# Attention and token/channel mixer on one core: a shorter opening in one PSUM bank, bfloat16 fillers, the identities behind the first load, and batch 2's second token product in seven products

## The chip, the cores and the metric

The kernel runs on one core of one Trainium2 chip. The metric is the device time of one execution in microseconds; the lower the better. Where several runs are shown, the median counts.

## The reference

The inputs are q, k, v (8 batches, 8 heads, 1024 positions, 64 features), E and F (64 x 1024) and four weights of a mixer. In fp32:

```
k_proj = E @ k;  v_proj = F @ v                     # per batch and head: 64 x 64
attn   = softmax(q @ k_proj.T / sqrt(64))           # 1024 x 64
x      = heads of (attn @ v_proj) side by side      # 1024 x 512 per batch
h      = relu(x.T @ w_tok1) @ w_tok2                # token products: 1024 -> 256 -> 1024
u      = x + h.T
out    = u + relu(u @ w_ch1) @ w_ch2                # channel products: 512 -> 1536 -> 512
```

## The kernel before

All products run in bfloat16 with fp32 sums in the eight PSUM banks. Loads by GpSimd (POOL) turn fp32 into bfloat16 on the way.

**Stages.** For a batch there is a front and a back. The front: `kv_proj` (line 509) multiplies k and v by E and F, `k_transpose` and `q_transpose` turn what the scores need, `scores` (line 613) gives q·k and its exp goes to `a` on ACT (line 622), `attend` (line 636) multiplies by v, and DVE divides by the sum (lines 648 and 653). Then come the first token product (`token1...`), the second (`token2...`) with x added on DVE to give u, and the turning of u. The back: `up_set` (line 1172, three sets in each half batch) and `down_block` (line 1281). The channel products use the seven-product scheme of Strassen and Winograd: seven products of quarters for eight, with sums of weights and operands on DVE and ACT copies of a PSUM bank that seed the next sum.

**The second token product in three forms.** Batch 0 works by pairs of heads (`token2_part`). Batch 1 uses eight plain sums of 512 columns (`token2`, lines 727 and 738). From batch `TWO = 2` on, `token2` calls `token2_two`: rows by two, 4 times 4 products of 512 columns (line 752) and a DVE sum of 1024 elements (line 765). From batch `T2 = 3` on the form is `token2_seven`: four DVE differences of 256 (line 961) and two sets, each with seven pairs of products of 256 columns (line 983), one ACT copy (line 1025) and six DVE sums of 512 (lines 1013 and 1019). It needs four sums of weights, `tok2_sums` (line 935), which are made after the back of batch `T2 - 1`.

**The order.** Every piece of work is a job of a planner, with an engine, its reads and writes and its PSUM bank. The planner does not choose: the order of all jobs is written out by hand in the string `ORDER` (two characters a job), and the bank of each in `SPOTS`. The instructions of each engine run in just this order. A job's place in it is called its place below. Loads of batch 0 are by two heads each, in the order of their jobs on POOL's queue.

**The opening.** After the zero tiles are set, PE runs ten bfloat16 products of 512 columns on zeros (`warm`, line 422), one into each bank and three into bank 7. The jobs that take a bank depend on all of these and on `identities`, which makes a bfloat16 and an fp32 identity on POOL. With the fp32 identity PE turns E and F (line 447), and ACT and DVE copy them to `EFT_sb` (line 450), which every projection needs. The tuple `FILLS` names places of PE jobs; ahead of each such job, once for each time that it is named, stands one more product on zeros, in fp32 (line 1516, two records each in the profile):

```python
FILLS = (20, 25, 25, 25, 25, 25, 25, 38)
```

Place 20 is the turning of E and F, place 25 the first projection (heads 0-1), place 38 the first score. POOL issues the loads of k 2-3, v 0-1, q 0-1 and k 0-1, makes the identities, and goes on with v 2-3, k 4-5, v 4-5, q 2-3 and so on.

Of the kernel before, what the change touches and what calls it, by code (L numbers as in the profile page):

```python
# [12 lines left out]
ACT = mybir.ActivationFunctionType  # L13
EARLY = 12.0
ORDER = (
    "0301020P0U000W0V0X0R0Q0T0Z040607050Y090S0a0b0c080d0y0z141M100+0-15110A0B1312161O1P1Q0C1N1R18171m1U19"
    "1S1A1n1o1q1B1T1p1r1D2A1J1E1C1K1V0D1t1s2C2B1F1W1Y1u1X1Z1L1v1G1H1a1j2J1d1w2G2K0E1g0F1b1c1e1k1f1l1I1y0G"
    "1x2H2I1z2D2N1h2L24271i2F2E2O1+2125282Y2629221-2V2g2M2b2h2c232P2d0I0H202W2Z2Q2R2X2S2l2i2m2e2n2q2T2a2j"
    "2o2f2k0J0K2U0N0O2v2r2z2p2w2+0L2s2t312x2u2y2-350e32393336303D370f3A3Z3r34383L0g3V3a3X3B3W0i3b3M0j3C3c"
    "3d3e3E3H0k0m3Y3s473f3g3t3v0h3x3h3i3j3F3l3u3w3y483I3G3k0n0o3m3N494B3J3z4A3O0u0l3n3Q3-4C4q4P3+3K404E4F"  # L20
    "4D4m0p4r4Q413P0M4o4G4H3R3o4n4J4u4s424I4v4R4K0v434w616562634p4L3p4x564X660w4Y4y4+4N4t646857676B0q4z0r"
    "3S3T0s45504Z4M693U6C4U6A6X4V516V6Y6T6W5A6f5844464S6U6g4-526c6h5B4W6D6i536j5D0t596Z4T5O5E6F3q6H6G6E6a"
    "6d6b6e0x6L5G6p6q4O6M6r6I4a6K5H6J5C6kAF5P6l6N4b5Q6O6m5F5S5T6v6s6x5IAH4c6w6t4e6y6u6+6n5J5V4f6-6z5R6o70"
    "4d7971735U5W7A4i76545g74757E725X775K7H4j787F7B7I7G5Y7J7N5h6R6P6SAKAJ7K7CAL7D7O7Q7P7L7R5a7M7W7T6Q7S5b"
    "7X5c5LAG4k7U5i7VAN557Y5e5d4g5Z5M5N7ZAP7bAO5l7a7c7d7fAQAR4l7e7g5m7o7k7i4h5oAS5n7p7lAI7j5r7m7n5pAXAYAZ"
    "Ab5s7hAcAa5jAj5qAd5f7vAg875t7rAkAeAhAf7w5vAoAt5w7x7yAi7tAp7zAuAqAvAwAl5x5kAM7+AmAxArAn80AyAV88AsA-7s"
    "AzB08189A+8AB57-B65uB17u8BBFB28382AUBDBG5zB38CB4BEB78P84BHB8BABIB985BJBK8QBL8E8R7qBR8TBBBM8FBCBNBUBO"
    "BS86BV8S8U8H5+8D8WBPBW8X8hBTBQBb8ZBXBYBc8i8aBZBd8GBf8JBa928IBeBg5-948K8jBhAWBi968pBl8VBj8L97Bk9A8qBm"
    "938YATBn98Bo8r8b8N8cBp9KEWEVBq605yBr999B8d8f958MEZ9C9DBs9L9OBtEb8m9E9PER8eEd8gEa9GBu8n9HEc9FBw9RBx9I"
    "ByEX9S9J9Q9M9c9N9d8oEeBz9UB+Bv9T9e8s9fB-9g9W9X8tEl8kEnEm9iEj9Y8uEY8OC1Es8lEh8w9V9hEkEoEt9j8vEp9aEqEr"  # L30
    "C3C5C6C49k8x8+C9CAEu8-C7C89lEvEwCC9mEg8yC29nEzCDE+F0E-9u908z9oF19vCFCBExCJ9wEyC09pCKA0Ei9ZEf9qCEF2F3"
    "9sF4CHCIA1CLF5F6CN9zF7IaFA9rCMCO9+A2CQFBF8F9FC9-FDCbCRCPCGFE9tCSA3DEFFCcA4CVFGFH9b9xA5FI9yCTCfA7FJFK"
    "CgA6FLCdDGCWFPCiABA8DIIdCXFNFOA9DHCeFMCjCUDJFQETFRChFTFSCYFUDFCkDMACFVFZFWFXDNClESCnFaADFYFdIhCmAAIZ"
    "FhFbFeCoFcDPCtFfEUCZCpFiIgDKFkFmIeFjCuDODLFlCrDQCqCvFoDSIfFnC-DTCyD0FwFgFpDRFrFqDUFt91FxD1CzDWFzFsFu"
    "DoDVCsFyCwDXDaF-DYF+C+IbDbDZG1D2G0DdG2G3D3CaG4G6DpG5DsIiFvDqG7DcG9DeDgIrIsIpDfIqCxD4GBDiDtDrD6InDjIo"
    "DhD7IwDvDwIxItD5DADuGDIcI-DkGAIuD8IvDBGEIyDxGFIzI+DyGHJ1DCJ2J3J0IlGGGIDzGCD+D-E0E4GKE5GLE6J4J6E2J7Dm"
    "GNGRGJE9J8GMGOJ9JAGSEAGPJBIjJ5DlJCECD9JEAEJDEDJGGVJFGQEBJHJIEEDnGXG8GWEFE1GYJJGTGUGZJKEGGjJLE3GkGaEH"
    "E7JMImJNE8JOGnGoEJGdGbGqJPJRJSGeHNEIGcJTJUEKHMELIkMhJVGpGlJWJQGfHOHQJYGmGrJZGsENJXJdGvJaMjMiJbJeMkJc"
    "EOGtMmMdMeJlGgJhGwJfG-HRJiEPGhHSJjJgHPJmMgGuMfHTDDEMMlJoGxH0JkJqGiJnHUH1HWGzJpH4JsHVHXJrJtJ+H5JvHYGy"
    "JuJwJ-H7HaHbJxK1H8HZH2JyH9H6K2HeK0HcJzK3HfHAHgK5K4HdHiHBK6HwHjHhG+HCK7K8HlH3MnMoMpKAK9KDHxKBHmH+HkHo"  # L40
    "KFMrHEH-MtHnHqI1HrHDMsHpMuKHHyKGHFMxI2HsMyHzKEMzHII0KIKJMvI3M+KLI6MwM-KKHGI7HJI4KMN0N3ICHKN1N2HuKON4"
    "N8HHI8IAKPEQIDN5KCI5IEI9KRKVKNN6N7KQIHN9NDNAKSIINBNCIKKWNINEILKTNJIJIBHtHvNFKXINIMKUNGNHKnKZIOIFNKKo"
    "IPKaMqKYLQNLNMIGQhKcKrKdNNKpKbIRKsNONPNQIQNRNSISIVKeLSNXKuQiKfITKvNYKqKgQlNTNVNZNWLRNULTNaIWKhKtQmNc"
    "NdKiKwIXLUKxIUNbLVNeKjNhKzQnKyQoK+NfKlNgNiLWL3NlK-NjNpLYL4NmNkNnLXNqNsO2QpL1NuNrLaL2NtNvQkLZNwQjNoL5"
    "LbNxNyO3L8O7O5LcQqNzLeN-LdL9N+LfLgO0LiO4O6LBLALjO9O1KkLmLkOAL0OBLCOCLnLpLELqIYHLKmOEO8LFLlOFR2LsLoLD"
    "LGL6QzR3ODQxLIQvLtOHLJLhQ+LrQwQyL+LuLKQ-OLR0L-M0M1M2R1OJR4LvL7M3R5R6LHQrQtLLM4M5OMR9RARBM6OPLMOQM7ON"
    "OSMGMAM8OIMBOOR7LNMCOKM9R8MERCOZMHRDLwLORERFRGOTORMIOaOVLyOUMDOGMORHMPOdOWRIObOeRJMLOXMQOgPURKRLMFRO"
    "OrOYLxOcQuRMRPRQMMMNMJOsRNRROtOhMROjMSRSRTLzMTOfRUQsUmOiMKMVRVOlOuOvRWMUOwOkOmUlRbMWRXOyPYRZRcMZRaMX"
    "RdOxRePZUpOnOzRYOpRgUqRhPWRfPaO+UtRlUsRmUrMYPcRiPVP1OoRjO-RkPXRpMaRnP2PdRtRqOqRoP7RrMbRsP3PbP0UoS6Ru"
    "P8PfRwPeP5P9S7RyRxPCRzMcPgR+PhPFRvPkUuR-PiP4PDS0S1LPS3PGS9PjSBPmPlPES4SAPIPnS2P6UnSDS8PoPqPAPJSCSESF"  # L50
    "SGPrPpPtSIPBUzPHQ2PuU+Q3PwSJSHPsUvUxPxUyUwPKPLQ4Q6PMQ7S5U-PvQ5SLSPV0PyV1SQQ9PNV4QAPzSMPOV5PQQCQ8V6SN"
    "P+QKV7V2SRSTQDV8QBQEV3V9QLSUSWPRQ0SSQMVCQFSXQGVAVDVBSVQIQHSOSYQSVEQTPPVHSbVFVIVGPSVJQPSdQUVMSeScVKVL"
    "QQSKSZQRSfP-ShVOSvQVVPVQSaSgSiTYSkSwQJVNSxVRQWSzSjSlVSVTQ1S+SyQNVUT0SmQXQOVVSnSpTcQYTaVWQZT1SoVXT3Qa"
    "QdVbSqQbTdVcTBQcTeTgVZVaT4VdVYTbTZS-VfVeTfThVgQeT2VhTjVlViTkQfSrVjT5PTT6VkTmVmTqVtTnT7StVpT9TCTrVqTA"
    "VuVnTDTiTuVoTvTlSsVrTJVyTsToVsTGVwTpTxTyU6TtTHU7T+TKVzSuT8VxV+TIVvV-UATMTLW0W1TNW6W3TwW2W4T-TEW7W9TO"
    "TzWATFTQUBW5U0W8TRWBWDTPU1WEU8UDUCTUUEWFTSWCUFWGUGU9UOTVUHTTQgWLWHWPUIWQTWWNWdWeUPUJWTU2UKWOUQWIWRWf"
    "WMWUUWWgWSWWWhWVWjUXWiUMWJU4WkWXUTWlWYWZWKUUUYWnWmU3WbWvUVWaWoUZWwWpWzULUaURXZXYWcWqU5UbW+W-UNX0XcUS"
    "UdWxX1XaWrWyWsX2UcUeX3UhXdXeXgUiUfX5WtXfX4XhXBXjX6X7XkXbX9UjXCXiXuXDXmXlXGXvXoXHXyXpYAXnXwXzYBXxXJUg"
    "UkXITXYEX-X+YCY0WuYDX8Y1XqXKXMY4YFYHYGXAXNY5Y6YIXEY2YJXsXOXFXQYMY3Y8XPXRXLYSY7XSYNYOYQXTXtXUYTXVYKYU"
    "YXYLXrYYYPXWYZYVXXYaYWYdYRYiYbY9YcYlYfYgYeYqYjYkYnYmYrYsYhYoYuYvYtYp"  # L60
)
SPOTS = (
    "4217334766020247420761132347234101643701627014360774066762735213041450123142432343067765566765675675"
    "7567665777566576556567655413242211542021305213425767576575576676565577667573666650513140231414232503"
    "2032577665666567656666350675601421450140231314531504176766565656765666645267564312325051413232020302"
    "0477666765656566666745067565435152311422050530134126576676766666566675626736503245300142350321031412"
    "667767666565656666475765703552043505304132314120375"
)
# [116 lines left out]
def kernel(  # L185
# [232 lines left out]

    def blank(b):
        nc.tensor.matmul(  # L422
            b, zero, zero[:, None, :].to_broadcast([P, NJ, P]), start=True, stop=True
        )
# [1088 lines left out]
    for place, j in enumerate(plan):
        if j.eng == "PE":
            for _ in range(FILLS.count(place)):
                nc.tensor.matmul(  # L1516
                    spare, zero32, zero32[:, None, :].to_broadcast([P, NJ, P]), start=True, stop=True
                )
# [40 lines left out]
```

## Time and profile before

| | |
|---|---|
| median of 3 runs | 421.67 us (421.25 to 421.83) |
| profiled execution | 421.36 us, span 419.6 us |
| PE busy | 411.8 us, 98% |
| DVE busy | 353.0 us, 84% |
| ACT busy | 229.6 us, 55% |
| POOL busy | 66.8 us, 16% |
| chain that ended last | PE 96%, ACT 3% |
| lines of that chain | L1172 35%, L1281 35%, L867 4%, L983 4%, L509 3%; L1516 1%, L422 1% |

PE is TensorE, PEld its weight loads, DVE VectorE, ACT ScalarE, POOL GpSimd. L12 is line 12 of the kernel before. An engine's time is a sum over stages that differ; a stage is read from its own stretch of the trace. Times in the trace count from the start of the span. The records of one engine overlap a little, so the spacing of two starts says more of what an instruction costs than its length.

### The profile page before, as it was taken

The numbers are of one execution on the slowest core, as the hardware profiler recorded it, in microseconds if no ns is written. First come the engines' busy times: TensorE is split into PE (matmuls) and PEld (weight loads), VectorE is DVE, ScalarE is ACT, GpSimd is POOL, SyncE is SP. The second block draws the span as 40 slices with busy tenths as digits, with TensorE's granted clock in tenths as the row PEclk, the third lists the DMA queues.
The fourth block names the chain that finished last, engine by engine and source line by source line (L and its number), as shares of the span: only waits on it lengthen the run. The fifth ranks groups of instructions, "written<-read, shape, count | busy, mean of one in ns | idle before, by whom it ended". The sixth has DMA issues, their size and how long they took to land.

```text
span 419.6 us, 9401 instructions
## 1 busy us (share of the span) xinstructions
PE 411.8 (98%) x3830; PEld 348.6 (83%) x3830; DVE 353.0 (84%) x748; ACT 229.6 (55%) x444; POOL 66.8 (16%) x105
## 2 busy tenths in 40 slices
PE   9889999999999999999999999999999999999996
...
DVE  2169978989879899989898889989998988889685
ACT  1767895457466456663746547573736645354620
...
DMA  8999999997999779969859698859772401250314
GB/s 153 206 201 205 206 203 161 202 170 116 213 211 183 123 140 167 176 170 194 182 98 208 125 195 201 130 123 173 154 165 81 59 27 76 50 151 2 153 50 152
DMA packets 96812, 62.48 MB, mean 149 GB/s; under 512 B 62080, under 2 KB 92288, under 8 KB 96768
## 3 DMA queue, kind: packets, MB, share of 16 engines
...
q1 hardware_dynamic: 61056, 16.00, 23.6%
...
q8 instruction: 30, 0.49, 0.5%
q14 instruction: 14, 0.11, 0.1%
HBM read 59.24 MB, written 16.78 MB: 181 GB/s over the span
## 4 chain that ended last, share of the span: by engine, by line
PE 96%; ACT 3%; DVE 0%; issue 0%
PE psum L1172 35%; PE psum L1281 35%; PE psum L867 4%; PE psum L983 4%; PE psum L509 3%; PE psum L613 3%; PE psum L672 2%; PE psum L1516 1%; PE psum L422 1%; PE psum L636 1%; PE psum L1084 1%; ACT qT L605 1%; PE psum L727 1%; PE psum L1052 1%; PE psum L703 1%; PE psum L752 1%
## 5 line engine op out<-in xcount | busy, mean ns | idle before, releaser
L1281 PEld LDWEIGHTS <-G 128*128 128x128 bf16 x1344 | 130.2, 98 | 18.0
L1281 PE MATMUL psum<-wc_sb,G 128*128 128x256 bf16 x768 | 104.0, 273 | 0.0
L1172 PEld LDWEIGHTS <-wc_sb 128*128 128x128 bf16 x768 | 73.8, 98 | 10.3 <-issue 0.4
L1281 PE MATMUL psum<-wT,G 128*128 128x256 bf16 x576 | 78.3, 273 | 0.0
L1194 ACT ACTIVATE G<-psum 128x512 bf16<-128x512 f32 x96 | 57.0, 601 | 29.6 <-PE psum L1172 29.4
L1208 DVE TENSOR_TENSOR G<-G 128x512 bf16<-128x512 bf16 (+1 forms) x140 | 70.0, 515 | 0.6
L1172 PEld LDWEIGHTS <-wT 128*128 128x128 bf16 x576 | 55.8, 98 | 7.9 <-issue 0.4
L1172 PE MATMUL psum<-S,wc_sb 128*128 128x256 bf16 x384 | 57.1, 273 | 0.0
L1172 PE MATMUL psum<-uT,wc_sb 128*128 128x256 bf16 x384 | 56.4, 273 | 0.0
L1172 PE MATMUL psum<-S,wT 128*128 128x256 bf16 x384 | 56.2, 273 | 0.0
L622 ACT ACTIVATE a<-psum 128x512 bf16<-128x512 f32 x64 | 36.8, 599 | 23.7 <-PE psum L613 23.0
L1315 POOL DMA_DIRECT2D out_dram<-o x30 | 16.3, 547 | 182.7 <-DVE o L1321 133.5
L1200 ACT COPY ua<-psum 128x512 f32<-128x512 f32 x48 | 28.2, 587 | 28.3 <-PE psum L1172 28.0
L1321 DVE TENSOR_TENSOR o<-psum,u 128x512 f32<-128x512 f32 x59 | 40.1, 683 | 3.0 <-PE psum L1281 2.5
L1200 ACT COPY ub<-psum 128x512 f32<-128x512 f32 x48 | 28.3, 590 | 24.5 <-PE psum L1172 22.9
L1153 DVE CUSTOM_DVE_ANT_0 G<-psum,ub 128x512 bf16<-128x512 f32 x48 | 32.8, 684 | 8.5 <-PE psum L1172 8.5
L1215 ACT COPY psum<-psum 128x512 f32<-128x512 f32 x48 | 27.7, 577 | 19.7 <-PE psum L1172 12.1
L1153 DVE CUSTOM_DVE_ANT_0 G<-psum,ua 128x512 bf16<-128x512 f32 x48 | 32.8, 684 | 4.9 <-ACT ua L1200 3.9
L344 POOL DMA_DIRECT2D v_sb<-in_v_dram x18 | 13.4, 745 | 111.2 <-DMA uT<-u 50.3
L1172 PE MATMUL psum<-uT,wT 128*128 128x256 bf16 x192 | 28.8, 273 | 0.0
L689 DVE TENSOR_TENSOR x_sb<-psum,rdn 128x512 bf16<-128x512 f32 x40 | 27.6, 690 | 1.2
L613 PE MATMUL psum<-qT,kT 128*128 128x512 bf16 x64 | 22.3, 379 | 0.5 <-ACT kT L560 0.4
...
## 6 DMA issues: line engine op xcount, KB each, us to landing
...
```

What stands on the lines that cost most here:

```text
L613: lambda: nc.tensor.matmul(bank(bk), kT[:, h].rearrange("p c k -> p (c k)"), qT[:, h].rearrange("p j s -> p (j s)"), start=True, stop=True,),
L622: lambda: nc.scalar.activation(out=a_t[h // 2 % 2][:, h % 2], in_=bank(bk), func=ACT.Exp, scale=scale),
L689: lambda: nc.vector.tensor_tensor(out=x_sb[:, :, h * D : (h + 1) * D].rearrange("p (n c) d -> p n c d", n=2), in0=view()[:, :, :, 0:D], in ...
L867: nc.tensor.matmul(to, tok1_of(n, si), mv, start=(n == 1 and si == 0), stop=(si == NJ - 1), skip_group_check=True,)
L1153: nc.vector._custom_dve(TENSOR_ADD_SAT, out=out, in0=in0, in1=in1, s0=FMAX, s1=0.0)
L1172: nc.tensor.matmul(t[:, c, :], w1_of(n, dd, 2 * m + c), a_of(j, n, dd), start=(n in (1, 7) and c == 0 and dd == 0), stop=(c == 1 and dd == 1),
L1194: lambda: nc.scalar.activation(out=G[:, n, cs], in_=view(src), func=ACT.Relu),
L1200: 512, lambda: nc.scalar.copy(out=dst, in_=view("y")), writes=[(name, s % 2)],
L1208: 512 * len(both), lambda: f(out=G[:, n, c], in0=G[:, a, c], in1=G[:, b, c]), ps=False,
L1215: 512, lambda: nc.scalar.copy(out=view("y"), in_=view("x")), takes=[bk["y"]],
L1281: nc.tensor.matmul(to, G[:, G_OF[n], cc, t * P : (t + 1) * P], w2_of(n, cc), start=(n in opens and (t == 0 or alone) and cc == 0), stop=(c ...
L1321: 512, lambda: nc.vector.tensor_add(out=dst, in0=view(src), in1=u_of(sh, dh)),
```

## The change

- The opening has four products on zeros, two bfloat16 and two fp32, all into bank 5; only bank 5 counts as written at the start.
- The fillers are bfloat16 products on zeros, 21 of them: 1 ahead of the turning of E and F (place 6), 1 ahead of the first projection (11), 7 ahead of the turning of q 0-1 (15), 2 ahead of the projection of heads 2-3 (18), 3 ahead of the first score (30), 2 (41), 2 (60) and 3 (87) further on.
- `T2` is 2: batch 2's second token product takes the seven-product form, and `tok2_sums` follows the back of batch 1.
- `ORDER` and `SPOTS` are written anew for the whole program. Among what moves: POOL makes the identities right behind the first load; the loads come as k 0-1, v 0-1, v 2-3, q 0-1, k 2-3, q 2-3, q 4-5, k 6-7, k 4-5, v 4-5, q 6-7, v 6-7, then the token weights in the same order; of the six loads of `w_ch1` those of the second group come first; the first load of batch 1 (v) now stands ahead of the `w_ch2` loads.

```diff
 ORDER = (
...
 SPOTS = (
...
-FILLS = (20, 25, 25, 25, 25, 25, 25, 38)
+FILLS = (6, 11, 15, 15, 15, 15, 15, 15, 15, 18, 18, 30, 30, 30, 41, 41, 60, 60, 87, 87, 87)
 WHOLE = 3
 TWO = 2
 T1 = 2
-T2 = 3
+T2 = 2
...
-        done, held, clean = set(), {}, [True] * 8
+        done, held, clean = set(), {}, [i == 5 for i in range(8)]
...
-    def blank(b):
-        nc.tensor.matmul(
-            b, zero, zero[:, None, :].to_broadcast([P, NJ, P]), start=True, stop=True
-        )
-
-    def warm(i):
-        return pe(
-            1, 512,
-            lambda: blank(banks[i]),
-            prio=-200, writes=[("bank", i)],
-        )
-
-    opening = [warm(i) for i in (*range(8), 7, 7)]
+    def blank(z):
+        nc.tensor.matmul(
+            banks[5], z, z[:, None, :].to_broadcast([P, NJ, P]), start=True, stop=True
+        )
+
+    def warm(z):
+        return pl.add("PE", 0.43, 0.43, lambda: blank(z), prio=-200)
+
+    def warm32():
+        return pl.add("PE", 1.71, 1.71, lambda: blank(zero32), prio=-200)
+
+    opening = [warm(zero), warm(zero), warm32(), warm32()]
+    for j in opening:
+        j.mms = 1
...
-    spare = banks[5]
     for place, j in enumerate(plan):
         if j.eng == "PE":
             for _ in range(FILLS.count(place)):
-                nc.tensor.matmul(
-                    spare, zero32, zero32[:, None, :].to_broadcast([P, NJ, P]), start=True, stop=True
-                )
+                blank(zero)
             pin()
```

More of the change, by code (lines that the diff above doesn't have):

```diff
@@ L15 @@
 ORDER = (
[L16 to L60, printed above, removed]
+    "0P0Q0R0S000T0W0X010U0V0s0402030+0t0u1G050w0v080x0-1H0z0y1I1J1012091O06071114151P1L1o0A1M1K0B1N1S2413"
@@ new lines @@
+    "1p1T0C0D251Q0E161R261g1A171D1h1j1X181E1B2A1i1C190H0I2D1F0G1k2C2B1l1Y1Z1m1n1s1U2E1V1W1q1a1d2H1b1t2F1r"
+    "1c1e2G1f271u28291v1+211x2V2a2W1w1y1-20222b2I1z2P2Q232J2X2f2c2Y2g2K2R2L2d2M0F0J0K3K2h2S2e2i2k2t2l2N2T"
+    "2U2Z2O2u2p2j2m332n2o2q340L0N2v2x0c2y2r2-3B2z302s2w3F310d2+323T3U3l350Y0Z363P0a413R3Q0e3V3W3X3C0b3G3S"
+    "3r373Y3m3D3a0g383n3b3p3Z3o3q3E3d3c39423s0h3t0i3f3g3u3H3J3e0M433A0f4547463I443v504g483x4J0O494B4i3w3y"
+    "4A0j3z3h4h4C4k4l5x5y515-4D5+4m3j3-4E0k4o4K4p5z4L520o4F0l0m4j0p544n553L4r4R60570q534S3M4H614s653N4T4q"
@@ new lines @@
+    "6258634t66644u4O566R6S6N6O6P4w4P6T594x3i4Q6U6V675C3+4v3k4G6B5I3O6Z4U6Q686W4M696a5D6A6C5J6L6M6J6F6D4V"
+    "6E406X6G6b6Y4y0r0n6c6H6I5M6d4W4I4N6e5A5N6h6mAAA96n4Y6i6f6o5K6j6p6g6k6u6l6v4Z5P6r6w4X6s6q4z5B5Q706x6t"
+    "6y5O4c5L6z73745R715S5a6+72787B6-5E5T755b4d79767A7C777D7E7H5UAI6K7I5c5i7F7J7G7K7L7N7Q7M7O7R7P5FAB5G7S"
+    "AL4e4a7V5V5WAK5Y5Z5H4+AP5j7W5X7T7XAM7UAN7YAO5f7Z7e5g7g7a7iAH7f5h7h7c7d5dAJ5l5k7j4-AQAVAX5mAhAWAY4b5e"
+    "AjAi7bAZAaAb7p5nAC7q81Ae5pAT7lAc7nAkAdAfAm7r7tAgAnAoAl5q7s5oAuAxAp7u825r7wAy7kAq7mAR85B0AvAw7vArAUB1"
@@ new lines @@
+    "B25t83Az867xB584As7oAtBBBC887y7-A+B67z89BDA-B7B8B380BE7+8J878BB4BMBFB9BA8ABG8KBJ8NBNBHBK8D8LBIASBPEj"
+    "BOBLBQBSBTBR8O8CBU8Q8P5u8R8MBVBXBZEk4fBa8b8T8EBY8UBb8y90BW8cBc8SBeBd918+8VBf925vBg948W95BhBj8zBk8-AD"
+    "8X9EBi9697BlBn9F9G8FEn93988ZBm99AF8HBo8d9CBr8gBp9I8h9H9DAEBsEp8aBu8jBwAGBq9JElErEqEo9A8k5s9BC4Bv8GBy"
+    "9L8Y8e9MBxBz8lBtC5B+B-C08i9O9W8IC99P9XC7C18fC28mEs9KC3C89a8nCB9bC69N9Q8oCCEv9Y8q9ZCDCA9R9dCEF4CGCH5w"
+    "8r9c8pE-F5ExEz9e9fEm8s9g9hE+9S8u9iCN8v9j9oCJEyF0COCLCFF1CRCPCS9kF29pCQF99qFACIF39UF69mF7CbF8CU9wFBCM"
@@ new lines @@
+    "8wFCCc9xFE9tCd8tCVFDCeFG9y9TFHCtCXFFCYCu9uEwFICK9lFOFJCTCfFP9nCWEt9vCxCvCgFKFLCZCiFMFNCaDWCy9z9VFQ9+"
+    "9rChFRFSC+9-CjCkFTFUCwC-CzA1FV9sCnA2ClD0D3FWCoA0CmD9A3FXA5D1DaFYFdFZD4A6FbDYD2FcDZFaA7D5CpD6DbFeDAFf"
+    "DeDcFgFiFhEuFjDBFkD7DdDfIrFlDhFnIoA4D8IvDXFmFpDiA8In8xCrFoItIsCsFqDgDHFvDjFrFsFwIuFtDEDoFyF+DkFzDlDF"
+    "G0F-DGG1DpDmFxDIDsG2FuG3DnDJDtCqG4DKDqDvDLIpIwG8DwG9G5G6DyDuGBDMGCDCDrE4GAGFDzGDDDDODxE5GGGHD+GKG7GI"
+    "E8E9GEDNJ8E6DPD-EBGLJ9I-E7ECDQDSDREAE0EEGJJ0GRJ3J1EDEGJ4E2GNGSEFGPDTJ5J2GTEMGVIqJ6GUEHJ7GQENGWDUJAJD"
@@ new lines @@
+    "EOJBGfGgEIGYJEJCEUJFEVEKELE1GOJGJHJIERGhGjGZJJJKESEWGiEJJLJSGXGkJME3JPEPGbJTGaJNGdGmIzJQETJRGeIxJOEX"
+    "GxGMJUGcGyGnJVJWDVI+IyGlEYG-GzH0JXGpG+GoEQMsMrHaGrEZEbHeH2GqJYHcJZGsJaEcEaHfHiEfHgHbJbHjHlJcHdH3JhH5"
+    "JdJfEdHhHmJiH1HoHDJjJgJeEgH6JlJkHpJmHEMtMuJnGtGuHkH4EhGvH7JoJpH8JqHsJrJzJsJtH9HnJvHBJuMvHFHqJwJ+JxGw"
+    "HCHrK0HtHLMxK1J-K2HIK4HMEeEiK3HAMzMwK5JyHuHwKCHNK6MyHxKDK7HJHvK9HGKHKFKAHyHzHKH+KGHOK8KJKEHHM+I0I1KK"
+    "KBH-I8I2HPKLI3I9KOHQIAIEICHRKPHSKMKIIDHTM-N1KRIBIFHWN7N3HXN8IGI4N4KNIQNCIINDHUKTKUI6IHHYIRN9KVIJN5IK"
@@ new lines @@
+    "KSNAISIYNBKWHVILIMN6KZNEKXNHIZNFKbKaKcIOINNINGNJIVKdNRNSIWNKI7NLKeKfKjIXNMKhIbKgKkNNKnNOKYKlKiKmIaK-"
+    "IcNPNQI5KoNTL0KQNWNXITNUL3NVLeIdNYIPIUKqIfNZKpKrL4KtL1NaNbKsLgIgIeN2N0QvNcL6KvNdIjKuNeL7L2KwLiL9IhNf"
+    "NgLhLjL5LHNiNhL8LAIkLmNlLnNmLkQwLINjNkQxKxNnLpLBNoNqQzNpIlLJLCNrLqLfKzR1NsLPKyNvNtNwLDNzNuLQLoLFNxLs"
+    "LEN+Q-LMR0IiLlLrQyNyO1LwLNHZO2N-K+LRO0LOO4O6LuO5LxLvLtL+LSO8O3O9O7LTLKLyQ+L-OAOBLUOGLzOCM1ODM2R2OEOI"
+    "OHLLM0OJM4LVOKM5OLLGLaONM3MCOOOPMDLbLWMGOSOMOTRGMEOQRHLXLcOFOVLYMFMHRBR7OZR9M6OROXImM7RCR8MIRDRERAOa"
@@ new lines @@
+    "MJMURLObMKMMM8RFOYMLOdRIMAOcRMMNRJMORQMVRKMPOeMWLdLZR5OnRNOoOgOUROOWMQMSMcOrMdRPRRMRMeRVOpRSOhOjOqOs"
+    "RTOkOfRUOiMZRXP3MaOlP4R4MBOuR6M9RWMbRYP5P6OvP7MfOmRZRcMgRaP8RdOxReMTOyPARbOtRfMhRgOwPiMXRhP9PmOzPBMY"
+    "O+MjMiPDRiPCR3U+RjPkPEMnPLO-RkRlMkMlPnPFRpPqPMRnMoRmPGRoRqRrV1PNPrRsP1PHPtRuPoRtPuRvRzPTV5V3MpV4R+V2"
+    "PJPjRwUzMmPsRxPUPIPpRyP+P0S5R-PvS1PVS2P-S6PlPQS3P2S0PyS8PRS9PzSAQ2PwS4SCS7Q0Q3SBSDSKPOSEPxQ5SLSHSFPK"
+    "PSSISNSPQ6Q1PWQ8SOSGPXPPQGSMSRPYQ4PZPaSSQ9Q7V6U-PeSJV0STPbQHQKPcSWQASXSQPfQIQBQLPgQCQNQEQOQJV9VBSUQM"
@@ new lines @@
+    "V7VCVAV8QQQYQPSZQRVGSbQZSVVDVHQaSdQSVLVEVFQgVIQTQUQhVJVMSeVQQWVKVRMqSrSfQiSsVNShVVQdVOVPSaQXScSvVSPd"
+    "StSgSiSjVTQDVUQVSwQeSySuVXSkQfVWQFSxSzVYQbSlS-VZVcS+VdVeQjSYSmSnT1TmT2QkVfSoSpVaQcT7VgToQlQnVhVbT0T8"
+    "ViQoQmTnSqVjTpTBTqTDVkQpT9TCVpTEQrVlTrVnTATFVqVmTsTuVoVrTvTtVtQsTHT3TGQtTJVsVuTwVvTKTxVwTPTyVzTIVxT+"
+    "V+VyTQW5PhQqT-TLW6TzV-W1TNT5TRQuW0TOW2U2W3U0WAU3TUU6W8TVU4TXW4W9WBTMT4U7TWWCW7WKTYU5U9TaWDWEU1UAWFTb"
+    "U8WHUCWLTZWGWPWNUDWITSUKWOTcUBTTT6WRWMULUOUMUETeUPUNWSUQTdURTiTfWTUSWQUFUTWWWUWJUcUUTgWVWZWbWaTjWdUW"
@@ L61 @@
+    "UVTkWeUdUXUGUeWhWrWfUIUkWsWtWiWvUlWXUJUYWkUaWgUmWcWYWwWyWjX7WlWzUhWuThWmW-WpWnWqUiX8X0XDXBUjUHWoXCWx"
+    "W+UnX9XEUoUZUfX1UgUpUbXFXAUrXGXqX2UqXmXJUsXPXHX3XKUvXoXLXNUtXrXsXuY6X5UwXtXIXQXvUuTlY7XRXxY8XnY9YAXy"
+    "XXXwXYXMYBXpXOUxXZXzX4X6YDXUYOX+XVYEYPYQX-Y0YCXWYFYRUyXaXSY1YSXbYIYTXTY2XcYUYVYJYgXdYWXeYXXiYKYaY4YM"
+    "YbXfXgYhYcXjYGYiYeYYYlYmXhYHYZYLY5Y3YNYfYdYnYwXkYkYoYpYjYqYrYzYtXlYsYuZ2Y+Z3YxYyZ4Z0Z6Y-Z7Z5YvZ1"
 )
 SPOTS = (
-    "4217334766020247420761132347234101643701627014360774066762735213041450123142432343067765566765675675"
```

9 lines of the change are left out of this document (5 added, 4 removed).

## The prediction

> **What bounds the kernel now.** I read the 40-slice strip first, then the chain of waits of the first 60 us, the issues of POOL and ACT's timeline in the opening, and last the busy time by stage.
>
> ```profile
> PE   9889999999999999999999999999999999999996
> DVE  2169978989879899989898889989998988889685
> ACT  1767895457466456663746547573736645354620
> DMA  8999999997999779969859698859772401250314
> ```
>
> PE is full except in slices 2 and 3 and the last. I compared the start of each matmul with the start of the one before it plus its own stream time (columns / 2.4 GHz + 2.5 ns, the pitch that the dense stretches show: 0.109 us for 256 columns, 0.216 for 512). From 40 us to the end there is no positive remainder. So the time is the time at which PE becomes dense, plus the PE work left, plus a tail. Only two things can change it: PE work, and idle or filler time ahead of 40 us. A new stall later would be the third.
>
> The chain of waits in the opening:
>
> ```profile
> 1.00 4.45 PE psum L422 x10
> 5.44 1.04 PE psum L1516 x2
> 6.48 0.88 PE psum L447 x8
> 7.37 5.15 PE psum L1516 x12
> 12.52 0.57 PE psum L509 x16
> ...
> 24.88 0.54 ACT a L622
> 25.50 0.26 ACT vb L522
> 25.77 0.27 ACT vb L522
> 26.06 0.61 ACT a L622
> 26.71 0.40 PE psum L636 x4
> ```
>
> To 12.5 us PE only multiplies zeros and turns E and F. Then ACT leads the chain almost without a break until the last exp (L622) at 26.06, and PE is dense from 26.7. What opens that ACT chain is the loads:
>
> ```profile
> 1.27 0.82 POOL L344 DMA_DIRECT2D k_sb<-in_k_dram  x1 [0.82 <-POOLq L1543]
> 2.09 0.74 POOL L344 DMA_DIRECT2D v_sb<-in_v_dram  x1
> ...
> 4.24 0.25 POOL masks.py:197 MEMSET ident<- 128x128 bf16 x1
> ...
> 5.30 0.72 POOL L344 DMA_DIRECT2D v_sb<-in_v_dram  x1
> ...
> 11.60 0.71 POOL L344 DMA_DIRECT2D v_sb<-in_v_dram  x1 [0.58 <-DMA k_sb<-in_k_dram]
> ```
>
> The landings in the trace come in the order of issue: 7.45, 8.73, 10.02, 11.31, 12.57, 13.86, 15.13, 16.43, 17.70, 18.98, 20.26, 22.40 us. In the plan the first four are k of heads 2-3, v 0-1, q 0-1, k 0-1. The first projection needs k and v of heads 0-1, so it waits for the fourth landing, 11.31, and then for the row of fillers, which runs to 12.5.
>
> **The change, part by part.**
>
> *Loads and identities.* The new order is k 0-1, identities, v 0-1, v 2-3, q 0-1, k 2-3, q 2-3, q 4-5, k 6-7, k 4-5, v 4-5, q 6-7, v 6-7. The identities take POOL from 4.24 to 5.30, 1.06 us, and now stand ahead of eleven loads. The second load is issued at 3.15 and not 2.09, and its 0.74 us are over by 3.9. The first load's issue ended at 2.09 and its first packet moved at 3.98, 1.9 us later, so the second can move from 5.8; the queue is on the first until 7.45. The later loads come 0.74 us apart where one takes 1.28 to land. The delay is hidden by the queue, and I keep the landings; unhidden it would be 1.06 us.
>
> *Opening.* Ten bf16 products 0.43 us apart (4.3 us) become two of these and two fp32 ones. [...] E and F landed at 4.46 and 5.65, so their turning starts near 5.9 in both, and EFT is ready near 7.7 (8.1 before). Nothing waits for it.
>
> *Fillers.* Eight fp32 ones (8 x 0.86 = 6.8 us) become 21 bf16 ones (21 x 0.216 = 4.5 us): 1 ahead of the turning, 1 ahead of the first projection, 7 ahead of q 0-1, 2 ahead of k/v 2-3, and 10 in four later gaps. All lie in gaps that the walk below shows open.
>
> *The walk* (landing to PE 0.24 us, as from F at 5.65 to the weight load at 5.89; ACT steps at their spacing in ACT's timeline: 64x128 copies 0.27, qT 0.93 to 1.02, exp 0.49 in a row). First projection at 8.73 + 0.24 = 8.97 (before 12.45), its four copies done by 10.8. q 0-1 lands at 11.31, turned by 12.2, copied by 13.2. k 2-3 lands at 12.57, projected by 13.45. ACT then has three copies, kT ready at 14.3, first score at 14.35 (before 15.84). From 17.1 ACT is dense: exp, qT, two exps, two copies to 19.9; k/v 4-5, landed by 18.98 and projected by 19.87, then four copies and four kT copies to 22.1, qT to 23.05, exps from 23.0, 23.5 and 24.0, two vb copies to 25.0, and the last exp at 25.0 to 25.6 (before 26.55 to 27.15). On PE the v projection of heads 6-7 (L509) starts at about 23.6, behind the scores that wait for qT; before it was 24.41. After it one attend waits for its bank until the exp of head 6 ends at 24.6: a stall of 0.3 us. From 24.7 PE is dense, because the first token product's pieces lie between the attends.
>
> So the start gives: 24.41 - 23.6 = 0.8; two score products (L613) that stood behind this projection are now ahead of it, 2 x 0.216 = 0.4; and the stalls behind it, 1.0 us before (0.2 at 25.8, 0.5 at 26.1, the rest up to 38 us), become 0.3. Together 1.9 us. Bounds: none of it, if ACT's chain ends where it does now; 2.5, if ACT keeps the 0.16 spacing that some copies have.
>
> Is the next thing late? Counting PE work on, the first up product comes at 33.2 (its weights, fourth in their group, land at 32.4), the first k/v of batch 1 at 44.9 (44.0), its q at 51.2 (50.35), its second k/v at 55.9 (55.5). All are met, the last by 0.2 us with the 0.24 taken off, so more gain than this would be given back to the loads.
>
> *Batch 2's second token product.* Out go 16 products of 512 columns (L752), 16 x 0.216 = 3.45 us; in come 28 of 256 (as L983 of batch 3), 28 x 0.109 = 3.05. PE gains 0.40 us in its dense part. DVE loses four sums of 1024 (L765, spacing 1.135) and gets 12 of 512 (L1013 and L1019, 0.60) and 4 of 256 (L961, 0.20): +3.46 us. Three of the four weight sums (L935, 3 x 0.335 = 1.0) move up from 152-155 us. ACT gets two copies more, 1.0 us, and has room.
>
> ```profile
> 100.00:110.00 10.00, 10.00 (x94) 8.97 (x92) 8.30 (x18) 5.02 (x12) 4.08 (x6) 1.00 0.86 139
> 110.00:120.00 10.00, 10.00 (x80) 7.14 (x79) 8.63 (x15) 6.12 (x11) 0.00 (x0) 1.00 1.11 244
> 160.00:170.00 10.00, 10.00 (x94) 9.15 (x93) 9.49 (x19) 5.62 (x11) 0.00 (x0) 1.00 0.94 151
> ```
>
> The columns are length, PE, weight loads, DVE, ACT, POOL. From 80 to 130 us DVE is busy 9.03, 9.04, 8.30, 8.63, 8.72: idle 6.3 us. It gets 4.5. That leaves 96% busy; from 160 to 170, with the same step for batch 3, it is at 9.49 and PE has no stall. I take no stall, with 4.5 us as the far end.
>
> *The clock.* The opening's products are 0.43 us apart and those after 5.7 us take half. Before, PE is never still from 1.0 to 14 us, and the thinnest stretch, 14.8 to 18.3, streams about half the time at full speed. After, PE waits 1.7 us between the turning and the first projection, and streams about 1.3 us between 5.7 and 9.1. No row here is as thin. By the nearest, 14.8 to 18.3, I take full speed; the other end is half speed from 5.7 to about 12.5. Then the projection (0.6) and seven fillers (1.5) take 4.2 us, q 0-1 is turned 1.6 us later, and up to 1.6 of the 1.9 us are gone.
>
> [...]
>
> **Sum.** -1.9 - 0.4 = -2.3 us. The order of the last down products and stores is as before, so the tail (415.5 to 419.6) stays. The profiled execution was 421.36 (span 419.6): 419.1 and a span of 417.3. Its median of three was 421.67, 0.3 above: 419.4.
>
> **Rivals.**
> 1. *The start gives little*: half speed through the first gap, or the stream of loads a little later than before, so that the second k/v of batch 1 holds PE. For it: thinner fillers, a margin of 0.2 us. Against: landings 1.28 apart whatever POOL does. Only 0.3 of 1.9 us are left, so -0.7: 421.0. Chance 0.15.
> 2. *Slower: DVE becomes the bound in batch 2's front*. Its 4.5 us of new work fall at 105 to 122 us, where the sums gate the banks of PE's next products. In 100 to 120 DVE idles only 3.1 us; if nothing moves out of it and the rest lies on PE, 1.4 us; if none of the work finds a gap, 4.5 us: -2.3 + 4.5 = +2.2, 423.9. It decides against the change once PE waits over 2.3 us. Against: 160 to 170. Chance 0.09.
> 3. *Not what it says*: the opening brings nothing, as ACT ends where it did, and the token product alone counts: -0.4, 421.3. Against: loads two steps sooner. Chance 0.06.
>
> The forecast has 0.70, with 418.6 to 420.3 as its own range (bounds of the start, 2.5 and 1.0 us). Rival 1 is mostly under 420.8. About 0.2%, 0.8 us, is what can be told from no change. Faster: 0.70 + 0.11 = 0.81; same 0.04 + 0.06 = 0.10; slower 0.09. The range runs from 418.6 to 421.0.
>
> **What would show it.** Right: first L509 product near 9.0, last exp near 25.6, dense PE from 24.7, no positive remainder after 40 us, 28 more L983 products, DVE near 9.5 in 100 to 120. Wrong: products of 128 columns 0.107 apart after 6 us; landings moved; idle PE ended by DVE near 105 to 122 us; idle PE before the second k/v of batch 1.

## The result, and the profile after

| | before | after |
|---|---|---|
| median | 421.25 us (420.74 to 421.83, 7 runs) | 420.17 us (419.51 to 420.56, 7 runs) |
| profiled execution | 421.36 us, span 419.6 | 419.51 us, span 417.7 |
| last product on PE begins | 415.18 us | 412.45 us |
| from there to the end of the span | 4.4 us | 5.3 us |
| DVE busy | 353.0 us, 84% | 356.8 us, 85% |

The ratio of the runs is 0.9969 [0.9959, 0.9979]: 1.1 us faster; the forecast was 2.3 us. Below line 422 the lines of the kernel after stand one higher than those of the kernel before (L509 is now L510).

The 40-slice strip of the kernel after, to be held against that of before:

```profile
PE   7999999999999999999999999999999999999995
DVE  2288988999999898898989898998898997988684
ACT  2858984375746456565356645564545555362520
```

PE has its only hole in the first slice (10.4 us each), from which the long fillers are gone; slices 2 and 3, at 8 before, are full. DVE's eighth to thirteenth slices (73 to 136 us) are all at 9; before they read 9 8 9 8 7 9.

The opening in PE's own timeline (start, length, then what ended the idle time before it):

```profile
5.74 1.14 PE L448 MATMUL psum<-ub,o 128*128 128x128 f32 x8 [0.61 <-issue]
...
7.55 0.24 PE L510 MATMUL psum<-k_sb,EFT_sb 128*64 128x128 bf16 x1 [0.46 <-ACT EFT_sb L451]
...
8.12 1.69 PE L422 MATMUL psum<-zero 128*128 128x512 bf16 x7
10.25 0.62 PE L598 MATMUL psum<-ident,q_sb 128*128 128x128 bf16 x8 [0.45 <-DMA q_sb<-in_q_dram]
```

The first projection (L510) starts at 7.55. Two things are ready just ahead of it: the copies of E and F on ACT, over at 7.50, which the profile names, and v of heads 0-1, landed at 7.49 (k at 6.21). Further on the chain of waits:

```profile
5.28 6.20 DMA k_sb<-in_k_dram
11.49 0.04 issue
11.53 0.64 PE psum L510 x16
...
13.08 0.58 PE psum L614 x2
13.66 0.46 PE psum L598 x8
14.15 1.01 ACT qT L606
...
22.37 0.56 PE psum L510 x8
22.94 0.71 PE psum L637 x8
23.65 1.01 PE psum L1053 x16
```

The first line is the load of k of heads 2-3, the fifth load, issued at 5.28 and landed at 11.49: the chain of the new start hangs on it. ACT leads from 14.15, the v projection of heads 6-7 comes at 22.37 (24.41 before), and from 23.3 on PE is dense. ACT's timeline has the last exp at

```profile
23.80 0.60 ACT L623 ACTIVATE a<-psum 128x512 bf16<-128x512 f32 x1
```

where it was 26.55 before. The busy time by stage, columns as in the prediction:

```profile
100.00:110.00 10.00, 10.00 (x92) 8.11 (x90) 9.76 (x23) 5.89 (x13) 2.64 (x5) 1.00 1.15 187
110.00:120.00 10.00, 10.00 (x94) 9.20 (x92) 9.13 (x18) 6.23 (x11) 0.00 (x0) 1.00 1.09 210
```

DVE (fourth figure of busy time) is at 9.76 and 9.13, PE full in both. L752 is gone and L984 has 168 products for 140.

**The tail.** The three last stores that SP issues, first in the kernel before, then after (start, time until the last of the three is issued):

```profile
412.41 4.36 SPq L1315 DMA_DIRECT2D out_dram<-o  x3
```

```profile
413.21 1.35 SPq L1316 DMA_DIRECT2D out_dram<-o  x3
```

Of the same kernel after, DVE's last sums:

```profile
409.04 0.76 DVE L1372 TENSOR_TENSOR o<-psum,o 128x256 f32<-128x256 f32 x2
...
412.76 0.42 DVE L1372 TENSOR_TENSOR o<-psum,o 128x256 f32<-128x256 f32 x1
```

Before, SP sent a 256 KB store at 412.41, then waited for the last two sums and sent 128 KB each at 415.94 and 416.33. After, the 256 KB store, whose two sums were done at 409.80, stands last: the two of 128 KB wait for the last sum (413.18) and go at 413.21 and 413.63, and the 256 KB go at 414.12 and land at 416.74, 3.56 us after the last sum (before: 418.58, 2.67 after it). PE ends its products 2.73 us sooner, the span ends 1.9 us sooner.

So the questions: does this order of stores alone account for the tail; which part of the new start gives the gain; why the loads landed 1.2 us sooner; and how much room DVE has left. In the expectations the letters of the theories are each text's own.

### The profile page after: what moved, and what is told of

It reads as the page before. It is cut to its first block, busy times and chain, and to the rows that moved or that the text cites. A ratio compares the mean times of both kernels' runs of the same rounds, so it can differ in the third digit from the quotient of the medians.

```text
span 417.7 us, 9441 instructions
## 1 busy us (share of the span) xinstructions
PE 409.2 (98%) x3843; PEld 348.6 (83%) x3843; DVE 356.8 (85%) x760; ACT 229.8 (55%) x446; POOL 66.7 (16%) x105
## 4 chain that ended last, share of the span: by engine, by line
PE 92%; DMA 3%; ACT 2%; POOL 1%; issue 0%; DVE 0%; POOLq 0%
PE psum L1173 35%; PE psum L1282 34%; PE psum L868 4%; PE psum L984 4%; PE psum L510 3%; PE psum L614 3%; PE psum L673 2%; DMA k_sb<-in_k_dram 1%; DMA kT<-kb 1%; PE psum L637 1%; PE psum L1085 1%; PE psum L1053 1%; PE psum L704 1%; ACT qT L606 1%; PE psum L598 1%; PE psum L1114 0%
## 5 line engine op out<-in xcount | busy, mean ns | idle before, releaser
L1173 PEld LDWEIGHTS <-wc_sb 128*128 128x128 bf16 x768 | 73.9, 98 | 10.4 <-issue 0.4
L623 ACT ACTIVATE a<-psum 128x512 bf16<-128x512 f32 x64 | 37.2, 601 | 19.0 <-PE psum L614 18.9
```

Source lines behind the costliest of these rows:

```text
L623: lambda: nc.scalar.activation(out=a_t[h // 2 % 2][:, h % 2], in_=bank(bk), func=ACT.Exp, scale=scale),
L1173: nc.tensor.matmul(t[:, c, :], w1_of(n, dd, 2 * m + c), a_of(j, n, dd), start=(n in (1, 7) and c == 0 and dd == 0), stop=(c == 1 and dd == 1),
```

## The experiments

**The kernel after, a second time**

> The changed kernel once more, as the control of the other runs on this chip and as a second trace. Theory A (PE's dense part starts 2 to 3 us sooner, and 0.8 us are given back in the last stores, which SP issues in another order): last product ends about 2.7 us sooner than before, end of the span about 1.9 sooner, time 1 to 2 us under the kernel before. Theory B (the start gains less than the first trace shows; that trace was a lucky one, with loads that landed 1.2 us sooner by chance): the first load lands near 7.4 us, as before, and PE's last product ends only 1.0 to 1.6 us sooner.

420.07 us (419.42 to 421.61, 11 runs), ratio 0.9974 [0.9961, 0.9987], span 417.7. The landings come at 6.22, 7.50, 9.07 and 10.36 us, the fifth at 11.71 (11.49 in the first profile), and the last 5.2 us are the same. The later experiments on the kernel after are held against this.

**The last stores in order of readiness**

```diff
-    "YbXfXgYhYcXjYGYiYeYYYlYmXhYHYZYLY5Y3YNYfYdYnYwXkYkYoYpYjYqYrYzYtXlYsYuZ2Y+Z3YxYyZ4Z0Z6Y-Z7Z5YvZ1"
+    "YbXfXgYhYcXjYGYiYeYYYlYmXhYHYZYLY5Y3YNYfYdYnYwXkYkYoYpYjYqYrYzYtXlYsYuZ2Y+Z3YxYyZ4Z0Z6YvY-Z1Z5Z7"
```

(`Yv` is the 256 KB store, `Z5` and `Z7` the two of 128 KB, `Y-` and `Z1` stores of ACT's queue.)

> The changed kernel with the last stores on SP in the order in which their data are ready: the 256 KB store first, then the two of 128 KB. Theory A: SP issues the 256 KB store near 410 us and not at 414.1, the last landing comes about 2.3 us after the last DVE sum and not 3.6, so 0.8 to 1.3 us faster than the changed kernel and 2 to 3 us faster than the kernel before. Theory B: the end is set by the last DVE sum whatever the order, within 0.3 us of the changed kernel.

418.79 us (418.04 to 419.64, 6 runs), ratio to before 0.9937 [0.9923, 0.9950], 1.28 us under the kernel after on the same chip. SP's timeline:

```profile
409.82 3.72 SPq L1316 DMA_DIRECT2D out_dram<-o  x3
```

The 256 KB store goes at 409.82, right behind its sums, and the two others at 411.90 and 413.21. The last product starts at 412.45 as before this edit, and the span is over 4.0 us later in place of 5.2. This is the best kernel of the study.

**The kernel before with the tail of the kernel after**

```diff
-    "YXYLXrYYYPXWYZYVXXYaYWYdYRYiYbY9YcYlYfYgYeYqYjYkYnYmYrYsYhYoYuYvYtYp"
+    "YXYLXrYYYPXWYZYVXXYaYWYdYRYiYbY9YcYlYfYgYeYqYjYkYnYmYrYsYoYuYvYtYhYp"
```

> The kernel before with one thing of the change alone: on SP's queue the 256 KB store of an earlier pair of sums stands behind the two 128 KB stores of the last sums, as in the kernel after, not ahead of them. Theory A (the tail's loss is this order of stores and nothing else): from the start of the last product to the end 5.2 to 5.3 us instead of 4.4, time +0.8 to +0.9 on before, near 422.3. Rival (the tail grew for another reason, as DVE or the landings of the last stores): 4.4 us and a time within 0.3 us of before, 421.4.

422.36 us against 421.48 of before (ratio 1.0019 [1.0005, 1.0033]); 5.3 us from the last product to the end. One store moved on one queue costs the 0.9 us, in this kernel too.

**The fillers of before in the kernel after**

```diff
-FILLS = (6, 11, 15, 15, 15, 15, 15, 15, 15, 18, 18, 30, 30, 30, 41, 41, 60, 60, 87, 87, 87)
+FILLS = (6, 11, 11, 11, 11, 11, 11, 30)
...
-                blank(zero)
+                blank(zero32)
```

> The kernel after with the fillers of before: eight fp32 products, one ahead of the turning of E and F, six ahead of the first projection, one ahead of the first score, in place of 21 bfloat16 ones. Theory A (the fillers set the start of before): six fp32 products of 0.86 us put the first projection at 11.8 to 12.5 us (after: 7.55), q 0-1 is turned behind it at 12.9 to 13.5 (10.25), first score at 14.5 to 15.5 (13.06), the last exp 1.0 to 2.0 us later, the time 421.1 to 422.0, which is +1.0 to +1.9 on the kernel after (420.07). Rival B (the fillers are hidden behind the loads, and the order of the loads gives the gain): first score within 0.5 us of 13.06, time 420.0 to 420.4.

422.10 us (421.64 to 422.54, 11 runs), ratio 1.0015 [1.0006, 1.0025]: the gain of the start is gone, and the time is 0.6 us above before, about what the tail costs. In its chain of waits the old row of fillers is back:

```profile
7.37 5.15 PE psum L422 x12
12.53 0.59 PE psum L510 x16
```

First score 15.89, last exp 26.64 to 27.23. Product for product, PE runs 2.79 us behind the kernel after at 45 us. Behind small waits of the kernel after, near 83 us above all, the distance is 2.46 us from 108 us on, and it stays so to the last product.

**The loads of before in the kernel after**

```diff
-    "0P0Q0R0S000T0W0X010U0V0s0402030+0t0u1G050w0v080x0-1H0z0y1I1J1012091O06071114151P1L1o0A1M1K0B1N1S2413"
+    "0P0Q0R0S030T0W0X010U0V02000s040+0t0u1G060w0v070x0-1H0z0y1I1J1012051O09081114151P1L1o0A1M1K0B1N1S2413"
...
-FILLS = (6, 11, 15, 15, 15, 15, 15, 15, 15, 18, 18, 30, 30, 30, 41, 41, 60, 60, 87, 87, 87)
+FILLS = (6, 13, 15, 15, 15, 15, 15, 15, 15, 18, 18, 30, 30, 30, 41, 41, 60, 60, 87, 87, 87)
```

(The second line only keeps each filler ahead of the product it stood ahead of.)

> The kernel after with the order of loads of before (k 2-3, identities, v 0-1, q 0-1, k 0-1, v 2-3, and so on); the short fillers, the opening and the token product stay as in the kernel after. Rival B (the order of the loads gives the gain): the first projection waits for the fourth landing, 10.2, and starts near 10.45 us (after: 7.55); behind it seven fillers, 1.5 us, and q 0-1 turned near 12.6 (10.25); first score near 15.4 (13.06), last exp 1.5 to 2 us later, time 421.5 to 422.0. Theory A (the fillers alone set the start): with short fillers the fourth landing is still early enough, first score within 0.5 us of 13.06, time 420.0 to 420.5. If this run and the one with the long fillers both lose 1 us or more, each of the two was enough to hold the start, and the change had to do both.

423.47 us (422.49 to 424.02, 6 runs), ratio 1.0048 [1.0033, 1.0063]: 3.4 us above the kernel after, more than either theory gave. The stretches of the start:

```profile
7.10:10.50 3.40, 0.00 (x0) 0.11 (x1) 0.00 (x0) 0.24 (x1) 3.23 (x5) 1.00 1.22 196
10.50:13.90 3.40, 3.37 (x22) 1.71 (x22) 0.00 (x0) 0.95 (x4) 1.82 (x3) 0.50 1.23 198
```

PE has nothing to do from 6.9 us until k of heads 0-1 lands at 10.49, and then the granted clock (seventh figure behind the length, 0.50) is at half from 10.52 to 13.93: the projection takes 1.06 us for 0.59 and the seven fillers 2.79 for 1.5. The first score comes at 16.72. So each half of the new start is worthless alone: with long fillers the early loads wait, and with late loads the short fillers leave PE idle until the clock falls.

**No fillers**

```diff
-FILLS = (6, 11, 15, 15, 15, 15, 15, 15, 15, 18, 18, 30, 30, 30, 41, 41, 60, 60, 87, 87, 87)
+FILLS = ()
```

> The changed kernel without any of the 21 fillers; the four opening products stay. If the clock needs them (rival 1 of the prediction), the projection of heads 0-1 or what follows runs at half speed (16 products over 1.0 us and not 0.57, q turned in 0.9 and not 0.45) and the time rises by 0.5 to 1.6 us. If gaps of under 2 us do no harm, PE stays at full speed and the time is within 0.3 us of the changed kernel.

421.89 us (420.45 to 423.41, 12 runs), ratio 1.0009 [0.9994, 1.0023], not to be told from before. The stretches:

```profile
6.00:9.50 3.50, 1.46 (x23) 1.11 (x21) 0.69 (x1) 1.53 (x5) 3.50 (x6) 1.00 1.22 194
9.50:13.00 3.50, 1.65 (x21) 1.51 (x23) 0.00 (x0) 0.81 (x1) 1.87 (x4) 0.51 1.24 205
```

The clock is full from 6.12, falls at 9.54 and comes back at 23.19: 13.65 us at half speed. The first score is at 14.75 (13.06 with fillers), the last product 3.0 us later. In the kernel after the fillers cost PE nothing that it could have used, and with them the clock stays full from 4.25 us on.

**The identities behind the fourth load**

```diff
-    "0P0Q0R0S000T0W0X010U0V0s0402030+0t0u1G050w0v080x0-1H0z0y1I1J1012091O06071114151P1L1o0A1M1K0B1N1S2413"
+    "0P0Q0R0S000104020T0W0X0U0V0s030+0t0u1G050w0v080x0-1H0z0y1I1J1012091O06071114151P1L1o0A1M1K0B1N1S2413"
```

(`0T` is the identities' job; the first two places in `FILLS` move with their products, to 9 and 13.)

> The changed kernel with the identities behind the fourth load on POOL, as before, all else in place. Theory C (the early landings come from the identities standing right behind the first load): the first load lands near 7.4 us and every later one 1.1 to 1.3 us later than in the changed kernel, and the time rises by 1.0 to 1.3 us, to about that of the kernel before. Theory B (landings differ by chance or by which heads come first): landings as in the changed kernel, time within 0.3 us of it.

419.89 us (419.46 to 420.58, 7 runs), ratio 0.9967 [0.9954, 0.9979]: no different from the kernel after. The first loads landed at 6.52 and 8.20 us, for 6.21 and 7.49: later, but not by the 1.0 to 1.3 us that the identities were held to cost. In the profiled execution (420.57) k of heads 2-3 landed 0.55 us later than in the kernel after, and the last exp stands 0.57 later.

**The kernel before, a second time, and with the identities behind its first load**

> The kernel before, profiled a second time, for its landings. Theory 1 (the later landings belong to the program before: what its engines and queues do in the first 6 us): the first load lands at 7.3 to 7.6 us and the second near 8.7, as in the first profile. Theory 2 (the rate of the queue in the first 6 us changes from execution to execution, and the four after-like profiles with 6.0 to 6.5 us were lucky): anything from 6.0 to 7.6 us. The time stays at 421.3 within 0.5 by both.

420.93 us (one run), landings at 7.01, 8.32, 9.64 and 10.87 us; the median of before in this series was 421.54.

```diff
-    "0301020P0U000W0V0X0R0Q0T0Z040607050Y090S0a0b0c080d0y0z141M100+0-15110A0B1312161O1P1Q0C1N1R18171m1U19"
+    "030Z01020P0U000W0V0X0R0Q0T040607050Y090S0a0b0c080d0y0z141M100+0-15110A0B1312161O1P1Q0C1N1R18171m1U19"
```

> The kernel before with one thing of the change alone: the identities directly behind the first load on POOL's queue, where they stood behind the fourth. Theory 1a (the identities, standing on the queue between the fourth load and the rest, are what slows the first loads): landings 1.0 to 1.2 us sooner, near 6.3, 7.6, 8.9 and 10.2 us. Theory 1b (they are not; the second experiment pointed there, where they stood behind the fourth load and the first load landed at 6.52 us): first landing again near 7.45 us. The time: the first projection waits for the row of fillers until 12.5 us whatever lands sooner, so 421.3 within 0.4 by both; over 0.8 us faster only if the landings, not the fillers, set the start of before.

421.41 us, ratio 0.9998 [0.9988, 1.0008], landings at 6.03, 7.29, 8.61 and 10.67 us. The rate of the transfers in 40 slices of the first 12 us, for before and for this kernel:

```profile
GB/s 0 0 0 0 0 0 0 232 123 341 355 273 273 133 140 154 157 184 103 72 96 109 188 212 201 208 198 198 201 201 202 208 208 205 198 208 205 201 205 198
```

```profile
GB/s 0 0 0 0 0 0 0 191 150 396 382 218 246 191 154 205 212 205 191 212 208 208 191 208 208 208 164 96 174 205 201 205 195 208 157 191 191 208 212 212
```

In before the rate sinks to 72 to 109 GB/s between 5.4 and 6.6 us; with the identities behind the first load that dip is gone (191 to 212). POOL makes them from 4.24 to 5.30 us in before and is done with them by 3.2 here. The dip is there in all four profiles with the identities behind the fourth load (lowest slice between 5.4 and 6.6 us 72, 82, 85 and 106; the fourth is the kernel before with the changed tail) and in none of the ten with them behind the first (lowest slice in the same stretch 174 to 201). The first landing is 6.38 to 7.45 us in the one group and 6.03 to 6.78 in the other. So the dip goes with the place of the identities, but the landings only in part: the groups overlap, and execution to execution they move by as much again. For the fifth load nothing of it is left: it lands at 11.87 to 12.57 in the four and at 11.49 to 12.62 in the ten. What links POOL's work to packets that are already queued is not shown. In the kernel before the landings are worth no time, as the first projection waits for the fillers until 12.5; the kernel after does follow them, as is shown below.

**DVE's room in batch 2's front**

```diff
+        def twice(f):
+            def g():
+                if b == 2:
+                    f()
+                return f()
+
+            return g
+
         def from_x(out, keys, src, sh, dh):
             dve(
-                512, lambda: nc.vector.tensor_add(out=out, in0=view(src), in1=part(x_sb, sh, dh)),
+                512, twice(lambda: nc.vector.tensor_add(out=out, in0=view(src), in1=part(x_sb, sh, dh))),
```

`from_kept` has the same edit. The second kernel has `if b == 2 and i == 0:`, the first set alone.

> The kernel after with all 12 sums of 512 elements from PSUM of batch 2's second token product done twice (the same result written again): 12 x 0.60 = 7.2 us more on DVE between 112 and 130 us. In the kernel after DVE idles 3.4 us from 80 to 140 us and 1.45 us from 100 to 130, and PE has no stall there. Theory A (DVE is near its limit there, the rival of the prediction that DVE becomes the bound being one step away): what finds no idle time lies on PE: 7.2 - 3.4 = 3.8 us up to 7.2 - 1.45 = 5.8 us, time 423.9 to 425.9. Theory B (sums run ahead of PE's need by several banks, and later idle time takes it up): less than 2 us, time under 422.1.

> As the run before it, but only the six sums of the first set doubled: 3.6 us more on DVE. Theory A: 3.6 us against 3.4 us of idle time from 80 to 140 and 1.45 from 100 to 130: +0.2 to +2.2 us, time 420.3 to 422.3. Theory B: within 0.3 us of the kernel after (420.1), no idle PE from 105 to 140 us ended by DVE.

Twelve doubled sums: 428.03 us (427.69 to 429.19, 5 runs), ratio 1.0170 [1.0153, 1.0187], 8.0 us above the kernel after. Six: 423.25 us (422.95 to 424.21, 6 runs), ratio 1.0049 [1.0037, 1.0062], 3.2 us above it. What PE's waits from 100 to 140 us say of the kernel with six (us in total, times, longest; the kernel after has none there):

```profile
PE psum L984 <- DVE a L1022: 1.3, 2, 0.9
PE psum L1290 <- DVE o L1330: 0.9, 1, 0.9
```

Both lie above what even the theory of a DVE near its limit gave. In the trace the repeat starts 0.72 us behind its sum, not 0.60: 6 x 0.72 = 4.3 us and 12 x 0.72 = 8.6. Of that 3.2 and 8.0 come back as time of the runs (in the traces PE's products fall 3.75 and 7.9 us further behind those of the kernel after between 108 and 153 us); the idle time of DVE takes up about 1 us or less, not the 3.4 that it has from 80 to 140. Part of that may be the longer chain from product to sum to product inside the set, which the edit lengthens too; the runs do not tell the two apart.

**q 0-1 as the third load**

```diff
-    "0P0Q0R0S000T0W0X010U0V0s0402030+0t0u1G050w0v080x0-1H0z0y1I1J1012091O06071114151P1L1o0A1M1K0B1N1S2413"
+    "0P0Q0R0S000T0W0X010U0V0s0204030+0t0u050w0v080x0-0z0y10121G111H1I1J091O060714151P1L1o0A1M1K0B1N1S2413"
...
-FILLS = (6, 11, 15, 15, 15, 15, 15, 15, 15, 18, 18, 30, 30, 30, 41, 41, 60, 60, 87, 87, 87)
+FILLS = (6, 11, 15, 15, 15, 15, 26, 26, 26, 26, 26, 26, 28, 28, 41, 41, 60, 60, 87, 87, 87)
```

> The kernel with the stores in order of readiness (418.79 in the first experiment) with one change of the start more: q 0-1 is the third load instead of the fourth (v 2-3 changes places with it); its turning, the turning of k 0-1 and the first two scores go ahead of the projection of k/v 2-3; of the fillers 4 stand ahead of q 0-1, 6 ahead of the first score, 2 behind. Theory A (ACT's chain from the first qT copy to the last exp sets when PE becomes dense): q lands at 8.8, turned 9.05, qT copy 9.7 (10.91 in the kernel after), first score 11.2 (13.06), and of the 1.2 us that ACT starts sooner 0.5 to 1.0 reach the last exp and the time: 417.8 to 418.3. Rival B (the loads of heads 6-7, or the loads of batch 1 that were met by 0.2 us, are next): under 0.3 us, time 418.5 to 418.9. Rival C (the clock falls to half speed in the thinner start): slower than 419.3.

419.31 us (418.55 to 420.28, 6 runs), ratio 0.9952 [0.9938, 0.9966]: no gain on the stores' kernel (0.9937 [0.9923, 0.9950]), rather a loss. The first qT copy starts at 10.16 (11.13 there), the first score at 12.00 (13.51), and yet the last exp runs from 24.20 to 24.79 (24.02 to 24.62). The chain of waits names what is next:

```profile
8.86 9.45 DMA v_sb<-in_v_dram
18.31 0.04 issue
18.35 0.63 PE psum L510 x15
```

The projection of the third pair of heads waits for its v, landed at 18.31. From the loads of the later heads on, ACT's earlier start is given back.

## Why the prediction was right in direction and half in size

The forecast was 419.4 and the result 420.17, inside the range of 418.6 to 421.0. The first profiled executions differ by 1.85 us, the second by 1.44. By the prediction's own steps, in us:

| step | predicted | first profiles | second profiles |
|---|---|---|---|
| start, to a dense PE | -1.9 | -2.9 | -2.2 |
| batch 2's second token product on PE | -0.4 | -0.4 | -0.4 |
| waits after 40 us | 0 | +0.6 | +0.35 |
| tail | 0 | +0.85 | +0.8 |
| sum | -2.3 | -1.85 | -1.45 |

In the first profiles the last product comes 2.73 us sooner, in the second 2.23 (412.52 for 414.75); with 0.4 of that from the token product (28 and 16 products at their pitch) and the new waits against it, 2.9 and 2.2 are the start's. That the result lies in the range is in part luck: a start that gave more than forecast paid for a tail and waits that the sum put at nothing. The run with the old fillers agrees with the first profiles: its last product is 0.27 us sooner than that of before, with the token product and two of the waits (0.34) in it, so its start is some 0.2 us better than that of before and 2.8 us worse than that of the kernel after: 3.0 together.

*Tail: wrong, and the step that cost most.* "The order of the last down products and stores is as before, so the tail (415.5 to 419.6) stays" is false: the order on SP's queue had changed, and one 256 KB store moved behind two that wait for the last sum. Two runs show it from both sides: +0.9 us in the kernel before, -1.28 in the kernel after. The queue's order could be read before the run, job by job.

*Loads and identities: wrong, and this is what made the start larger.* "I keep the landings" missed 1.2 us at the first load and 1.1 at the fifth, k of heads 2-3 (11.49 for 12.57). In the seven profiles that keep the new start with its short fillers (the identities late and q 0-1 third among them) the last exp begins 12.29 to 12.32 us behind this landing, wherever it falls between 11.49 and 12.43. (v of heads 4-5 lands 6.4 us behind it in all seven, so these profiles do not say which of the two holds; with q 0-1 third the chain names v.) With the landing kept at 12.57 these 12.3 us would put the last exp at 24.9, an estimate, where the prediction had 25.0. How much of the earlier landing was luck shows in the spread above: 11.49 is the earliest of all 14 profiles, and 12.57 one of the two latest.

*The walk: right in its mechanism, too late in its numbers.* First projection 7.55 for 8.97, since v of heads 0-1 landed at 7.49 for 8.73, together with the copies of E and F; q turned at 10.25 (the prediction's 12.2 is when it was to be done; the measured end is 10.9); first score 13.06 for 14.35; last exp from 23.80 for 25.0; PE dense from 23.3 for 24.7. From a landing to its first product it took 0.04 us, not 0.24: behind F in the kernel before, where the 0.24 was read, a filler was still running. The start gave 2.9 us for 1.9 in the first profiles, past its bound of 2.5, and 2.2 in the second. (By that bound of 2.5 the forecast's own range begins at 418.8, not at 418.6.) The kernel before moves too: its first projection begins at 12.45 where the clock rose at 5.68, and at 12.01 in its second profile, where it rose at 4.78. The fillers and the order of loads were counted as one; the runs show that both were needed.

*The loads next in line: right to be named, mis-sized.* PE lost nothing to the second k/v of batch 1. But the 0.6 us of new waits lie where the prediction had "no positive remainder" (gaps of 0.09 us, where PE goes from one kind of product to another, stand in both kernels): 0.27 at 83.3 us for the DMA transpose of kT, by the waits of the weight loads

```profile
PEld L614 <- DMA kT<-kb: 0.4, 1, 0.4
```

and 0.19 and 0.15 us at 303 and 326 us, two gaps for which the profile names no releaser but issue, and which stand in every kernel with the new order. The first comes and goes: none in the kernel's second profile, and with the identities late a wait of 0.6 us for a DVE sum (u, L739) stood in the same place.

*Batch 2's token product: right.* "I take no stall" held: no idle PE between 105 and 122 us, and 28 products came for 16. No run takes this part out alone.

*The clock: right.* It was full from 4.25 us on, and from 6.33 in the second profile. A fall to half speed behind the first gap, near to the far end of the prediction, is what happened with the loads of before and without fillers. The far end's 6.8 us of it, 5.7 to 12.5, were the author's estimate; the runs showed 3.41 and 13.65 us.

*The rivals.* The slower one, DVE as the bound, did not come, but stood closer than 0.09 suggests: 4.3 us more DVE work at this place made the kernel 1.8 us slower than before (423.25 against 421.48). The first rival's time, 421.0, is as far from the result as the forecast's, but its reasons (a lower clock, the loads) did not hold. The third is excluded: the start gave most.

One thing remains open: the profiled executions of the kernel after (419.51, 419.49) lie 0.6 us under the medians of its runs, that of before 0.1 over its own in one series and 0.6 under it in the other. The medians differ by 1.1 to 1.2 us. What the slower half of the runs of the kernel after loses, no profile of it shows. One candidate is the landing of k of heads 2-3, by which the start moved up to 0.95 us between profiles; another is the waits near 83 us, which differ between them too. Neither was tried.
